# A fused attention and expert kernel: the fourth attention unit's keys and queries loaded sooner, and in the experts the second-layer weight chunks behind all transposes, with later splits and squares

## The chip, the cores and the metric

The kernel runs on one core of a Trainium2 chip. The metric is the device time of one execution in microseconds. The core's engines work side by side, each through its own list of instructions in order: PE (matrix multiplication), DVE (vector), ACT (scalar functions), POOL (here indexed gathers and scatters) and SP (here only the issue of DMA transfers). They wait for one another through semaphores.

## The reference, cut to what matters

```python
# attention: q, k, v of shape (8, 8, 576, 64); heads 0-3 banded, heads 4-7 strided
scores = (q @ k.T) / 8
mask_local   = (rel >= 0) & (rel < 32)
mask_strided = (rel >= 0) & (pos_k % 32 == pos_q % 32)
x = softmax(where(mask, scores, -1e9)) @ v          # x: 4608 tokens of 512
# experts: 8 of them, each takes at most 576 tokens
logits = x @ w_gate                                 # (4608, 8)
for (token, expert) in order of falling logit:
    if token is free and expert has fewer than 576: assign
for e in range(8):
    out[mine(e)] = relu(x[mine(e)] @ w1[e]) @ w2[e] # 512 -> 1024 -> 512
```

## The kernel before, in words

**Attention.** Each of the 8 batches has a strided and a banded part; these 16 *units* (`todo[0]` to `todo[15]`, strided first) are worked through in pairs of heads, two per unit, by one loop over `i`. Step `i` computes head pair `i` (`mix`, `norm`), the scores of pair `i + 1` and the first matmuls of pair `i + 2`. Loads go over SP's queue in the order in which the code writes them: `load_kq` takes keys (`ks` strided, `kl` banded) and queries (`qs`, `ql`) of one head pair, `load_v` the values (`v_s`, `v_l`). All go through `flow` (L255 to L262), which makes the first transfer of a group wait for a given mark, an instruction of an earlier unit, or else for the third group before it. Some small constants are loaded between them: `wg_sb` (the gate's weights), `sum_g` and `desc8h`. `drips` are small instructions tied to a step; one copies `wg_sb` into `wgp`, at step `GW_AT - 1`.

**Who gets which token.** The logits lead to a search, expert by expert, for the 576th largest logit among the free tokens. A round of `search` is a chain across engines: DVE compares all values with 17 candidates (`cm`, L844), PE counts (nine matmuls, L860), DVE folds (`red`, `r`), PE sums (L869), DVE tests against 576 (`g`, L876), PE sums (L879), DVE forms the next candidates (`cand`, L882). The search for expert e + 1 and the work for it runs between the matmuls of expert e.

**An expert.** Its tokens are gathered by POOL in five chunks of 128 rows, the last of 64 (`xr`, L1109). `halve` (L1095) splits each chunk into a high and a low half-precision part: ACT writes the high one (`xg`, L1098), DVE the low one (L1099), and SP issues a transposing DMA into `xt` (L1100). The weights come in quarters (`w`, L1012); their scale is found by four squares per layer on ACT (`jk`, L1032), a sum on DVE (`ss`, L1040), a matmul on PE (L1042) and a few small DVE operations (`ss_e`, `w_sw`). Then `split` cuts each layer into eight pieces, a high one on ACT (`w1h`, `w2h`, L1052) and a low one on DVE (`w1l`, `w2l`, L1053), which reads the high one. The first layer is 192 matmuls of 288 columns (L1208, in `hidden`), whose results ACT and DVE split into `hh` and `hl`; the second is L1256 (L1250 for the last 64 rows), whose results `y` POOL scatters to the output (L1267).

**What sets the order.** PE's order is that of the code: `ffn` yields its matmuls with their cost, `clock` adds these up, and chains of other work (search rounds, squares, scales, pieces, gathers) are advanced when their due time on this clock has come; numbers such as `T_SCALE` or `T_W` are the steps between them. On DVE and ACT a scheduler orders by priority, `urgent` raises it, and `follow(ins, others)` adds that `ins` is placed after the others, an order only and no wait. `bulk` uses it to put an instruction behind the last finished search count (`sums`), and `counted` puts what was issued shortly before a count behind it. `rush` holds the experts whose first layer has been reached.

Of the kernel before, what the change touches and what calls it, by code (L numbers as in the profile page):

```python
# [13 lines left out]
OP = mybir.AluOpType  # L14
# [19 lines left out]
B_LATE, L_AT, G5, GW_AT = 5, 8, 6, 4  # L34
# [27 lines left out]
CUT0, T_BEHIND, ROWS_BEHIND = 1, 1300, 3  # L62
# [76 lines left out]
def band_stride_attention_then_capacity_moe(ctx, tc, qt, kl, ks, nl, ns, wg, w1, w2, cst, out, dbg=None):  # L139
# [82 lines left out]
    with tc.tile_pool(name="ld", bufs=2) as ld, \  # L222
# [369 lines left out]
        flow([(wg_sb, wg), (sum_g, cst["sum_g"]), (desc8h, cst["desc_h"])])  # L592
# [34 lines left out]
        for i in range(-1, 2 * nu):  # L627
            u, n, m = pair(i), pair(i + 1), pair(i + 2)
            nu_ = todo[i // 2 + 3] if i >= 0 and i // 2 + 3 < nu else None
            kq_ = todo[i // 2 + 2] if i >= 2 and i // 2 + 2 < nu else None  # L630
# [29 lines left out]
            if nu_ and i % 2 == 0:  # L660
                nu_.load_v(1, n[0].top)
            elif kq_ and i % 2:
                kq_.load_kq(1, n[0].top)
            if u:
                u[0].mix(u[1], 1)
# [75 lines left out]
    lately, sums = [], []  # L741
# [94 lines left out]
    def search(rm, ohc, more):  # L836
        cand, src, top = cand0, rm, None
        ohv = ohc.rearrange("p c e -> p (c e)")
        for rd in range(R1):
            last = rd == R1 - 1  # L840
            t = cand[:, :J1] if last else cand[:, 1:J1 + 1]
            with urgent():
                cm = rt.tile([TP, NC, J1], F16, name="cm")
                nc.vector.tensor_tensor(cm, src[:, :, None].to_broadcast([TP, NC, J1]),  # L844
                                        t[:, None, :].to_broadcast([TP, NC, J1]), op=OP.is_ge)
# [157 lines left out]
    def weights(ph, ei):  # L1003
        e = nc.sync.value_load(ei[0:1, 0:1], min_val=0, max_val=E - 1)
        res, todo = [], []
        for name, w, nch, width, bits in (("w1", w1, DC, FF, W1_BITS), ("w2", w2, FC, DM, W2_BITS)):
# [43 lines left out]
            def split(c, f, k, wf=wf, sc=sc, hi=hi, lo=lo):  # L1050
                s_ = sc.bitcast(F32)[:, 0:1]
                nc.scalar.activation(hi[:, c, f], wf[:, c, f], AF.Copy, scale=s_)  # L1052
                nc.vector.scalar_tensor_tensor(lo[:, c, f], wf[:, c, f], s_, hi[:, c, f], op0=OP.mult,  # L1053
                                               op1=OP.subtract)
# [25 lines left out]
        g = spread(ph, [(T_W, lambda: None)] + sq1 + sc1 + cut1)  # L1080
# [13 lines left out]
    def halve(ph, xt, xr, t, n):  # L1094
        xg = xp.tile([128, 2 * DM], F16, name="xg", bufs=5)  # L1095
        xs, xv = xg[:n].rearrange("q (a j d) -> q j a d", a=2, j=2), xr[:n].rearrange("q (a d) -> q a d", a=2)
        with urgent(ph):
            nc.scalar.activation(xs[:, 0], xv, AF.Copy)  # L1098
            bulk(ph if t < ROWS_BEHIND else 0, nc.vector.tensor_tensor(xs[:, 1], xv, xs[:, 0], op=OP.subtract))  # L1099
# [87 lines left out]
    def fetch(ph, slot, wts):  # L1187
        idx, sx = yield from indices(ph, slot)
        xt, todo = tokens(ph, idx)
        for t, f in enumerate(todo):  # L1190
            yield T_ROWS if t == 0 else T_ROW
            f()
            if t >= NT - 3:
                wts[2]({NT - 3: (0,), NT - 2: (1,), NT - 1: (2, 3)}[t])
# [99 lines left out]
    with tc.manual_schedule(engines=MAN):  # L1294
        work[0] = now[:4] + (now[4](),)
        chains.append([T_LOAD0, load0()])
        for ph in range(E):
            with tc.manual_schedule(engines=MAN0) if ph in MANP else nullcontext():
# [5 lines left out]
                lately.clear()  # L1304
                for c in list(chains):
# [77 lines left out]
```

## Time and profile before

| | |
|---|---|
| three runs | 675.93 us median (670.42, 676.23, 675.93) |
| profiled execution | 676.45 us |
| its span, first to last instruction | 674.7 us |
| mean granted clock of PE | 0.957 |
| PE busy | 603.6 us, 89% |
| DVE, ACT, POOL busy | 454.7, 332.6, 108.7 us |
| DMA | 102.40 MB, mean 152 GB/s |
| first layers (L1208), 1536 matmuls | 291.0 us of PE |
| second layers (L1256), 768 matmuls | 290.9 us of PE |

The busy times of matmuls overlap one another, since they are pipelined. In the rows below a time in square brackets is the idle time of the engine just before the instruction, with what ended it. "issue" means that nothing in the profile shows what the engine waited for; SPq is SP's queue of DMA issues.

### The profile page before, as it was taken

What the parts mean: (1) busy time and instruction counts of PE and PEld (TensorE: products, weight loads), DVE (VectorE), ACT (ScalarE), POOL (GpSimd) and SP (SyncE); (2) the same over time, 40 slices, a digit from 0 to 9 for tenths busy, and PEclk for the clock granted to TensorE, in tenths of its full rate; (3) what the DMA queues carried; (4) which work ended last, traced back from release to release, by engine and by line L of the source; (5) the groups of instructions that cost most, each with busy time, mean ns of one, the idle gap of its engine ahead of it and who ended that gap; (6) DMA issues with size and microseconds to landing.
All of it is one profiled execution on the core that took longest, in us unless ns stands there. A gap on an engine that the chain in (4) does not pass through costs nothing.

```text
span 674.7 us, 19417 instructions
## 1 busy us (share of the span) xinstructions
PE 603.6 (89%) x8128; PEld 395.4 (59%) x8128; DVE 454.7 (67%) x1381; ACT 332.6 (49%) x554; POOL 108.7 (16%) x124
## 2 busy tenths in 40 slices
PE   8789999998947699979999989989998999899993
PEld 4566667766733565457457448547646746646741
DVE  4757778877777888729768776975965956650600
ACT  2555554545302564535655456554565456843510
POOL 2001101111101100400330150051052031211011
PEclk9879999999966899979999999999999999899998
DMA  9868888887314503840590493375257089641010
GB/s 240 202 211 228 233 230 238 248 223 214 111 38 177 167 1 141 193 128 14 181 254 15 149 200 113 141 158 162 111 128 224 20 233 332 142 149 48 1 40 32
DMA packets 76363, 102.40 MB, mean 152 GB/s; under 512 B 41292, under 2 KB 49062, under 8 KB 75763
## 3 DMA queue, kind: packets, MB, share of 16 engines
q1 hardware_dynamic: 68195, 79.61, 41.7%
q0 software_dynamic: 7360, 21.15, 10.7%
q8 instruction: 64, 1.05, 0.7%
q10 hardware_dynamic: 720, 0.39, 0.2%
q14 instruction: 24, 0.20, 0.1%
HBM read 73.60 MB, written 18.87 MB: 137 GB/s over the span
## 4 chain that ended last, share of the span: by engine, by line
PE 17%; issue 15%; DVE 15%; DMA 10%; POOL 4%; ACT 4%; SPq 0%; POOLq 0%; DVEq 0%; ACTq 0%
PE ph L1208 12%; DMA w<-in_w_dram 5%; DVE w2l L1053 3%; PE ph L1256 3%; POOL xr L1109 3%; DMA xr<-x_scr,idx 3%; DVE hl L1216 2%; DVE w1l L1053 2%; DMA xt<-xg 2%; DVE cm L844 1%; ACT jk L1032 1%; POOL out_dram L1267 1%; DVE xg L1099 1%; ACT hh L1215 1%; DMA out_dram<-y,idx 1%
## 5 line engine op out<-in xcount | busy, mean ns | idle before, releaser
L1208 PE MATMUL ph<-xt,w1h 128*128 128x288 f16 (+2 forms) x1024 | 178.9, 290 | 6.8 <-DMA xt<-xg 4.8
L1208 PEld LDWEIGHTS <-w1h 128*128 128x128 f16 x1024 | 97.9, 99 | 36.2 <-issue 5.7
L1208 PE MATMUL ph<-xt,w1l 128*128 128x288 f16 (+2 forms) x512 | 112.1, 290 | 0.0
L1267 POOL DMA_INDIRECT out_dram<-y,idx x40 | 47.3, 1181 | 339.5 <-ACT y L1266 317.5
L1256 PE MATMUL ph<-w2l,hh 128*128 128x512 f16 x256 | 96.9, 379 | 0.4 <-DVE w2l L1053 0.4
L1256 PE MATMUL ph<-w2h,hh 128*128 128x512 f16 x256 | 97.0, 379 | 0.0
L1256 PE MATMUL ph<-w2h,hl 128*128 128x512 f16 x256 | 97.0, 379 | 0.0
L1032 ACT ACTIVATE jk<-w 128x1024 f16<-128x1024 f32 x64 | 67.4, 1054 | 56.5 <-DMA w<-in_w_dram 55.3
L1215 ACT ACTIVATE hh<-ph 128x576 f16<-128x576 f32 (+2 forms) x72 | 42.7, 592 | 81.9 <-PE ph L1208 81.1
L1256 PEld LDWEIGHTS <-hh 128*128 128x128 f16 x512 | 49.1, 98 | 57.4 <-issue 6.7
L1216 DVE SCALAR_TENSOR_TENSOR hl<-ph,hh 128x576 f16<-128x576 f32 (+2 forms) x72 | 49.5, 687 | 47.6 <-ACT hh L1215 47.3
L1208 PEld LDWEIGHTS <-w1l 128*128 128x128 f16 x512 | 50.7, 99 | 14.1 <-issue 1.4
L378 ACT ACTIVATE pr<-spa 128x576 f32<-128x576 f32 x32 | 20.8, 651 | 61.9 <-PE spa L375 45.2
L1053 DVE SCALAR_TENSOR_TENSOR w1l<-w,w_sw,w1h 128x512 f16<-128x512 f32 x64 | 46.1, 745 | 4.8 <-ACT w1h L1052 4.8
L1109 POOL DMA_INDIRECT xr<-x_scr,idx x40 | 41.5, 1038 | 46.8 <-DVE L L953 25.3
L1052 ACT ACTIVATE w1h<-w,w_sw 128x512 f16<-128x512 f32 x64 | 42.2, 710 | 13.0 <-DVE w_sw L210 11.9
L1266 ACT ACTIVATE y<-ph,so 128x512 f32<-128x512 f32 x32 | 21.8, 681 | 53.4 <-PE ph L1256 53.3
L1053 DVE SCALAR_TENSOR_TENSOR w2l<-w,w_sw,w2h 128x512 f16<-128x512 f32 x64 | 46.8, 746 | 0.4 <-ACT w2h L1052 0.3
L1052 ACT ACTIVATE w2h<-w,w_sw 128x512 f16<-128x512 f32 x64 | 42.2, 711 | 8.1 <-DVE w_sw L210 8.1
L1256 PEld LDWEIGHTS <-hl 128*128 128x128 f16 x256 | 24.9, 97 | 29.8 <-issue 4.0
L429 POOL DMA_DIRECT2D x_scr<-xs x23 | 15.1, 661 | 159.2 <-DVE vsum L298 101.7
L1099 DVE TENSOR_TENSOR xg<-xr,xg 128x512 f16<-128x512 f32 (+1 forms) x37 | 24.8, 685 | 15.1 <-ACT xg L1098 14.9
(619 smaller groups left out, 929.7 us busy)
## 6 DMA issues: line engine op xcount, KB each, us to landing
w<-in_w_dram SPq DMA_DIRECT2D x64, 512.0 KB
kl<-in_kl_dram SPq DMA_DIRECT2D x16, 304.0 KB
v_s<-in_ns_dram SPq DMA_DIRECT2D x16, 292.5 KB
v_l<-in_nl_dram SPq DMA_DIRECT2D x16, 292.5 KB
ks<-in_ks_dram SPq DMA_DIRECT2D x16, 288.0 KB
qs<-in_qt_dram SPq DMA_DIRECT2D x16, 288.0 KB
ql<-in_qt_dram SPq DMA_DIRECT2D x16, 288.0 KB
x_scr<-xl SPq DMA_DIRECT2D x8, 512.0 KB
```

Source lines behind the costliest of these rows:

```text
L378: nc.scalar.activation(pr[:, :S].rearrange("k (h n) -> k h n", h=2), u.sp[p][:, :, :HS], AF.Exp, scale=0.125)
L1032: ins = nc.scalar.activation(jk, wf[:, c * n4:(c + 1) * n4].rearrange("p c f -> p (c f)"), AF.Square, scale=1.41422, accum_out=sq[:, c:c + 1])
L1052: nc.scalar.activation(hi[:, c, f], wf[:, c, f], AF.Copy, scale=s_)
L1053: nc.vector.scalar_tensor_tensor(lo[:, c, f], wf[:, c, f], s_, hi[:, c, f], op0=OP.mult, op1=OP.subtract)
L1099: bulk(ph if t < ROWS_BEHIND else 0, nc.vector.tensor_tensor(xs[:, 1], xv, xs[:, 0], op=OP.subtract))
L1109: nc.gpsimd.indirect_dma_start(out=xr[:n], out_offset=None, in_=x_rows, in_offset=bass.IndirectOffsetOnAxis(ap=idx[:n, t:t + 1], axis=0))
L1208: nc.tensor.matmul(tile_[:, j, :w], wt[:, d, f * 128:(f + 1) * 128], xt[:, d // 2, xx, d % 2, c], start=(k == 0), stop=(k == 3 * DC - 1))
L1215: evicted.append(nc.scalar.activation(hv, src, AF.Relu))
L1216: nc.vector.scalar_tensor_tensor(lv, src, 0.0, hv, op0=OP.max, op1=OP.subtract)
L1256: nc.tensor.matmul(py, a[:, f, ts_], w[:, f], start=(k == 0), stop=(k == len(todo) - 1))
L1266: nc.scalar.activation(y, py, AF.Copy, scale=so[:, t:t + 1])
L1267: st = nc.gpsimd.indirect_dma_start(out=out_rows, out_offset=bass.IndirectOffsetOnAxis(ap=idx[:n, t:t + 1], axis=0), in_=y[:n], in_offset= ...
```

## The change

**Attention.** Keys and queries of the fourth unit (`todo[3]`, banded part of batch 1) are loaded at step 1, both head pairs, instead of at steps 2 and 3; the general rule starts at step 4. The three small constants go behind them instead of ahead of the loop, and `wgp` is copied at step 5 instead of 3.

**Experts.** (1) The quarters of the second-layer weights are issued by `fetch` after its last transpose, not between the last three. (2) In experts 1 to 6 the pieces from the seventh on (sixth on in expert 1), while the expert is not in `rush`, have their low part placed after the last finished search count, and pieces issued within 4000 of a count's due time are placed after that count. (3) The DVE half of the last row chunk is placed after the latest comparison `cm`. (4) The first layer's scale is due 2800 after its squares, not 1500, and the squares of expert 7's first layer start 15000 after its weights, not 4000.

```diff
--- before.py
+++ after.py
@@ -31,7 +31,7 @@
 OPEN_S, OPEN_L = 1, 3
 DEPTH = 3
 WARM = {(-2, 0): 11, (-1, 0): 3, (-1, 2): 3}
-B_LATE, L_AT, G5, GW_AT = 5, 8, 6, 4
+B_LATE, L_AT, G5, GW_AT = 5, 8, 6, 6
 V_AT, V_AT_S, COPY_AT = 5, 4, (-3, -5, -2, -4, -1, -4)
 VW = D + 1
 LR = 3 * 32 + E
@@ -59,7 +59,7 @@
 T_HOT6, T_CLOSE6 = 3200, 9000
 T_W21, T_SCALE2, T_CUT2 = (3200, 300, 3000, 3000), 2600, 1250
 T_F, T_LOAD0, T_HOT1, T_W, T_SQ, T_SCALE, T_CUT, T_BULK0 = 3000, 1500, 6350, 4000, 1500, 1500, 1500, 600
-CUT0, T_BEHIND, ROWS_BEHIND = 1, 1300, 3
+CUT0, T_BEHIND, ROWS_BEHIND, PIECES, T_TAIL, T_SCALE1, T_W7 = 1, 1300, 3, 6, 4000, 2800, 15000
 EDGE0, PEAKS, PEAKS_N = 18, (24, 29), (1, 3)
 FIRST_AT = (3, 4)
 LATE_Q, STORE_Q = (2, 3), (3, 4, 5)
@@ -589,7 +589,6 @@
         for p in range(2):
             todo[2].load_kq(p)
             todo[2].load_v(p)
-        flow([(wg_sb, wg), (sum_g, cst["sum_g"]), (desc8h, cst["desc_h"])])
         last = 2 * nu - 1
         edge = (B - 2) * S // TP
 
@@ -627,7 +626,7 @@
         for i in range(-1, 2 * nu):
             u, n, m = pair(i), pair(i + 1), pair(i + 2)
             nu_ = todo[i // 2 + 3] if i >= 0 and i // 2 + 3 < nu else None
-            kq_ = todo[i // 2 + 2] if i >= 2 and i // 2 + 2 < nu else None
+            kq_ = todo[i // 2 + 2] if i >= 4 and i // 2 + 2 < nu else None
             if nu_ and i % 2 == 0:
                 nu_.load_v(0, todo[0].top if i == 0 else todo[i // 2 - 1].done)
             late_constants(i)
@@ -661,6 +660,8 @@
                 nu_.load_v(1, n[0].top)
             elif kq_ and i % 2:
                 kq_.load_kq(1, n[0].top)
+            elif i == 1:
+                todo[3].load_kq(0, n[0].top)
             if u:
                 u[0].mix(u[1], 1)
             warm(i, 1)
@@ -674,6 +675,9 @@
                 u[0].norm(u[1])
             if kq_ and i % 2 == 0:
                 kq_.load_kq(0, u[0].done)
+            elif i == 1:
+                todo[3].load_kq(1, u[0].done)
+                flow([(wg_sb, wg), (sum_g, cst["sum_g"]), (desc8h, cst["desc_h"])])
             for f in mids3.get(i, []):
                 f(a, b)
             if n:
@@ -738,7 +742,7 @@
     def urgent(ph=1):
         return tc.high_priority(offset=URGENT * (2 if ph == 0 else 1))
 
-    lately, sums = [], []
+    lately, sums, cms, pieces = [], [], [], []
 
     def bulk(ph, ins):
         if ph and ph not in rush:
@@ -746,6 +750,10 @@
             lately.append((due_now(), ins))
 
     def counted(red, total):
+        while pieces:
+            t, ins = pieces.pop()
+            if t > due_now() - T_TAIL:
+                follow(ins, (total,))
         while lately:
             t, ins = lately.pop()
             if t > due_now() - T_BEHIND:
@@ -841,8 +849,8 @@
             t = cand[:, :J1] if last else cand[:, 1:J1 + 1]
             with urgent():
                 cm = rt.tile([TP, NC, J1], F16, name="cm")
-                nc.vector.tensor_tensor(cm, src[:, :, None].to_broadcast([TP, NC, J1]),
-                                        t[:, None, :].to_broadcast([TP, NC, J1]), op=OP.is_ge)
+                cms.append(nc.vector.tensor_tensor(cm, src[:, :, None].to_broadcast([TP, NC, J1]),
+                                                 t[:, None, :].to_broadcast([TP, NC, J1]), op=OP.is_ge))
                 cv = cm.rearrange("p c j -> p (c j)")
                 n = 1 if rd == R1 - 2 else J1 + 1
                 if not last:
@@ -1050,8 +1058,11 @@
             def split(c, f, k, wf=wf, sc=sc, hi=hi, lo=lo):
                 s_ = sc.bitcast(F32)[:, 0:1]
                 nc.scalar.activation(hi[:, c, f], wf[:, c, f], AF.Copy, scale=s_)
-                nc.vector.scalar_tensor_tensor(lo[:, c, f], wf[:, c, f], s_, hi[:, c, f], op0=OP.mult,
-                                               op1=OP.subtract)
+                ins = nc.vector.scalar_tensor_tensor(lo[:, c, f], wf[:, c, f], s_, hi[:, c, f], op0=OP.mult,
+                                                     op1=OP.subtract)
+                if ph and ph not in rush and k >= PIECES - (ph == 1):
+                    follow(ins, sums[-1:])
+                    pieces.append((due_now(), ins))
 
             todo.append([(T_SQ, lambda c=c, g=square: g(c)) for c in range(4)])
             todo.append([(T_SCALE, scale)])
@@ -1077,7 +1088,7 @@
                 return g
 
             return res, (start, more, later)
-        g = spread(ph, [(T_W, lambda: None)] + sq1 + sc1 + cut1)
+        g = spread(ph, [(T_W if ph < E - 1 else T_W7, lambda: None)] + sq1 + [(T_SCALE1, sc1[0][1])] + cut1)
         chains.append([due_now(), g])
         thirds[ph] = evenly([(t, f) for t, (_, f) in zip(T_W21, sq2)] + [(T_SCALE2, sc2[0][1])] + [(T_CUT2, f) for _, f in cut2])
         return res, g, later
@@ -1096,7 +1107,11 @@
         xs, xv = xg[:n].rearrange("q (a j d) -> q j a d", a=2, j=2), xr[:n].rearrange("q (a d) -> q a d", a=2)
         with urgent(ph):
             nc.scalar.activation(xs[:, 0], xv, AF.Copy)
-            bulk(ph if t < ROWS_BEHIND else 0, nc.vector.tensor_tensor(xs[:, 1], xv, xs[:, 0], op=OP.subtract))
+            ins = nc.vector.tensor_tensor(xs[:, 1], xv, xs[:, 0], op=OP.subtract)
+            if t < ROWS_BEHIND:
+                bulk(ph, ins)
+            elif 0 < ph < E - 1 and t == NT - 1:
+                follow(ins, cms[-1:])
             turned.append(nc.sync.dma_start_transpose(xt[:, :, t * 128:t * 128 + n], xg[:n]))
 
     def tokens(ph, idx):
@@ -1190,8 +1205,7 @@
         for t, f in enumerate(todo):
             yield T_ROWS if t == 0 else T_ROW
             f()
-            if t >= NT - 3:
-                wts[2]({NT - 3: (0,), NT - 2: (1,), NT - 1: (2, 3)}[t])
+        wts[2](range(4))
         yield T_LOAD - T_ROWS
         work[ph] = wts[0], xt, idx, sx, wts[1]
         ready.add(ph)
@@ -1302,6 +1316,7 @@
                     advance(c)
                 rush.add(ph)
                 lately.clear()
+                pieces.clear()
                 for c in list(chains):
                     if c[1] is work[ph][4]:
                         c[0] = clock
```

The rows show where instructions stand. First SP, attention, the loads of the third to fifth unit, as a difference (`v_l_147`, `kl`, `ql` are the fourth unit's, `v_s_139` the third's, `v_s_135` the fifth's):

```order
 L262 DMA v_s_139<-in_ns_dram 6x1560
+L262 DMA v_l_147<-in_nl_dram 32x2340 x2
+L262 DMA kl<-in_kl_dram 128x608
+L262 DMA ql<-in_qt_dram 128x576
+L262 DMA kl<-in_kl_dram 128x608
+L262 DMA ql<-in_qt_dram 128x576
 L262 DMA wg_sb<-in_wg_dram 128x32
 L262 DMA sum_g<-in_c_sum_g_dram 128x8
 L262 DMA desc8h<-in_c_desc_h_dram 128x8
-L262 DMA v_l_147<-in_nl_dram 32x2340 x2
-L262 DMA v_s_135<-in_ns_dram 48x1560
-L262 DMA v_s_135<-in_ns_dram 6x1560
```

The removed rows go on with the rest of the fifth unit's values and the fourth unit's `kl`, `ql`, `kl`, `ql`. These four stand ahead of the constants and of the fifth unit's values now.

SP again, the last stretch of expert 1's loading, before (`w_4794` are its second-layer quarters):

```order
L1100 DMA_TRANSPOSE xt<-xg 128x8x128 x3
L1012 ISA
L1012 DMA w_4794<-in_w_dram 128x2x512
L1100 DMA_TRANSPOSE xt<-xg 128x8x128
L1012 ISA
L1012 DMA w_4794<-in_w_dram 128x2x512
L1100 DMA_TRANSPOSE xt<-xg 128x8x64
L1012 ISA
L1012 DMA w_4794<-in_w_dram 128x2x512
L1012 ISA
L1012 DMA w_4794<-in_w_dram 128x2x512
```

and after:

```order
L1115 DMA_TRANSPOSE xt<-xg 128x8x128 x4
L1115 DMA_TRANSPOSE xt<-xg 128x8x64
L1020 ISA
L1020 DMA w_4794<-in_w_dram 128x2x512
L1020 ISA
L1020 DMA w_4794<-in_w_dram 128x2x512
```

All five transposes stand ahead of the second-layer quarters now, of which two are shown. In experts 2 to 5 that was the order before, too; in expert 6 it changes as here.

DVE, expert 3, from the first row chunk to the third round's comparison `cm`, before (numbers tell the chunks apart; `xg_6701` is the last one):

```order
L1099 TENSOR_TENSOR xg_6622<-xr_6557,xg_6622 128x2x256
L1099 TENSOR_TENSOR xg_6638<-xr_6559,xg_6638 128x2x256
L876 TENSOR_SCALAR g1_6630,ih1_6631<-pr__6602 128x8
L1099 TENSOR_TENSOR xg_6657<-xr_6561,xg_6657 128x2x256
L1099 TENSOR_TENSOR xg_6674<-xr_6563,xg_6674 128x2x256
L882 SCALAR_TENSOR_TENSOR cand18_6646<-steps_3772,pr__6602,pre1_6578 128x18
L1099 TENSOR_TENSOR xg_6701<-xr_6565,xg_6701 64x2x256
L844 TENSOR_TENSOR cm_6648<-rmn_6384,cand18_6646 128x612
L852 TENSOR_SCALAR pre1_6650<-steps_3772,cand18_6646 128x18
L1053 SCALAR_TENSOR_TENSOR w1l_6325<-w1_6317,w_sw1_6323,w1h_6324 128x4x128 x2
```

and after, where the last chunk is `xg_6697`:

```order
L1110 TENSOR_TENSOR xg_6620<-xr_6548,xg_6620 128x2x256
L1110 TENSOR_TENSOR xg_6636<-xr_6550,xg_6636 128x2x256
L1110 TENSOR_TENSOR xg_6655<-xr_6552,xg_6655 128x2x256
L884 TENSOR_SCALAR g1_6630,ih1_6631<-pr__6602 128x8
L1110 TENSOR_TENSOR xg_6671<-xr_6554,xg_6671 128x2x256
L1061 SCALAR_TENSOR_TENSOR w1l_6325<-w1_6317,w_sw1_6323,w1h_6324 128x4x128
L890 SCALAR_TENSOR_TENSOR cand18_6644<-steps_3772,pr__6602,pre1_6578 128x18
L1061 SCALAR_TENSOR_TENSOR w1l_6325<-w1_6317,w_sw1_6323,w1h_6324 128x4x128
L852 TENSOR_TENSOR cm_6646<-rmn_6384,cand18_6644 128x612
L860 TENSOR_SCALAR pre1_6648<-steps_3772,cand18_6644 128x18
L1110 TENSOR_TENSOR xg_6697<-xr_6556,xg_6697 64x2x256
L1061 SCALAR_TENSOR_TENSOR w1l_6325<-w1_6317,w_sw1_6323,w1h_6324 128x4x128
```

`cm` stands ahead of the last chunk now, and two pieces `w1l` stand between the fourth chunk and `cm`; `g` stands behind the third chunk instead of the second.

ACT at the same place, before:

```order
L1052 ACTIVATE w1h_6324<-w1_6317,w_sw1_6323 128x4x128 x5
L1266 ACTIVATE y_6591<-ph_6470,so_5973 128x512
L1098 ACTIVATE xg_6622<-xr_6557 128x2x256
L1098 ACTIVATE xg_6638<-xr_6559 128x2x256
L1098 ACTIVATE xg_6657<-xr_6561 128x2x256
L1098 ACTIVATE xg_6674<-xr_6563 128x2x256
L1052 ACTIVATE w1h_6324<-w1_6317,w_sw1_6323 128x4x128
L1098 ACTIVATE xg_6701<-xr_6565 64x2x256
L1052 ACTIVATE w1h_6324<-w1_6317,w_sw1_6323 128x4x128 x2
```

and after:

```order
L1060 ACTIVATE w1h_6324<-w1_6317,w_sw1_6323 128x4x128 x3
L1280 ACTIVATE y_6589<-ph_6470,so_5973 128x512
L1109 ACTIVATE xg_6620<-xr_6548 128x2x256
L1109 ACTIVATE xg_6636<-xr_6550 128x2x256
L1109 ACTIVATE xg_6655<-xr_6552 128x2x256
L1109 ACTIVATE xg_6671<-xr_6554 128x2x256
L1109 ACTIVATE xg_6697<-xr_6556 64x2x256
L1060 ACTIVATE w1h_6324<-w1_6317,w_sw1_6323 128x4x128 x4
L1280 ACTIVATE y_6660<-ph_6592,so_5973 128x512
```

Before, five pieces `w1h` stand ahead of the row chunks and one between the fourth chunk and the last; after, three stand ahead and five behind the last chunk.

## The prediction, made before the changed kernel ran

> **What bounds the kernel now.** I read the page first: the matrix engine (PE) is busy for 603.6 of 674.7 us, so it sets the time, and a change can only win where PE stands still or runs at the lower clock. Then I looked for PE's idle time, for what ended it, and for the granted clock around it.
>
> ```profile
> PE 603.6 (89%) x8128; PEld 395.4 (59%) x8128; DVE 454.7 (67%) x1381; ACT 332.6 (49%) x554; POOL 108.7 (16%) x124
> ```
>
> The rows of the second view cut PE's time into pieces of 3.41 us (the length of the shortest stretch at half clock), laid so that clock changes fall on their borders. Four places are shown: attention, expert 1, expert 3, experts 6 and 7. Columns: from and to, length, busy time of PE, PEld, DVE, ACT, POOL, granted clock, DMA share, GB/s.
>
> ```profile
> 36.89:40.30 3.41, 0.86 (x27) 0.70 (x27) 0.00 (x0) 0.60 (x2) 0.00 (x0) 1.00 0.96 350
> 40.30:43.71 3.41, 3.41 (x70) 2.91 (x70) 2.77 (x11) 1.84 (x3) 0.00 (x0) 0.50 0.20 70
> 43.71:47.12 3.41, 3.41 (x58) 3.00 (x56) 2.17 (x7) 2.74 (x4) 0.00 (x0) 0.50 0.59 178
> ...
> 286.06:289.47 3.41, 0.03 (x1) 0.00 (x0) 0.23 (x2) 0.12 (x1) 0.97 (x1) 1.00 1.10 290
> 289.47:292.88 3.41, 2.55 (x11) 1.65 (x12) 0.00 (x0) 0.00 (x0) 0.00 (x0) 0.50 1.07 403
> 292.88:296.29 3.41, 3.41 (x23) 2.36 (x21) 0.39 (x2) 0.00 (x0) 0.00 (x0) 0.50 0.00 0
> ...
> 395.28:398.69 3.41, 1.45 (x7) 0.49 (x5) 1.72 (x4) 2.12 (x5) 0.00 (x0) 1.00 1.14 202
> 398.70:402.11 3.41, 2.88 (x22) 1.42 (x23) 2.64 (x9) 0.50 (x1) 2.43 (x1) 1.00 1.18 194
> ...
> 576.19:579.60 3.41, 1.47 (x15) 0.96 (x13) 1.34 (x5) 3.38 (x7) 2.50 (x4) 1.00 0.71 204
> 579.60:583.01 3.41, 3.41 (x16) 2.16 (x15) 2.46 (x5) 2.14 (x5) 0.64 (x1) 0.50 0.75 196
> ```
>
> So PE's idle time is paid twice in places. A piece in which PE worked only 0.86, 0.03 or 1.47 us is followed by one or two at clock 0.50, each of which does half its work: about 1.7 us lost. The limit lies near 1.45 us busy: at 395 that much kept the full clock, at 576 1.47 lost it.
>
> The Trainium skill, "TensorE: Matmul & The Clock Gate" (Part 1, and "HAM oscillation"), has the clock as either half or full, decided over free-running windows of 3413 ns, which these rows show; but its rule asks for no idle gap above some 3.4 us, and the row at 576 lost the clock with 1.94 us idle. By that rule the clock term of the experts below would be nothing and the sum 2.7 us lower; the rows speak against it.
>
> **The change part by part**, against the profiled execution (676.45 us, span 674.7), 0.5 us above the median 675.93.
>
> *Attention: keys and queries of the fourth unit sooner.*
>
> ```profile
> 27.39 2.33 SPq L262 DMA_DIRECT2D v_s<-in_ns_dram  x4
> 29.82 0.35 SPq L262 DMA_DIRECT2D kl<-in_kl_dram  x1
> ...
> 37.50 0.43 PE L352 MATMUL spa<-ql,kl 64*64 64x32 f32 x16 [0.64 <-DMA ql<-in_qt_dram]
> 39.87 0.32 PE L352 MATMUL spa<-ql,kl 64*64 64x32 f32 x8 [1.93 <-issue]
> ```
>
> The four loads (SP ql and kl) leave the queue ahead of four v_s loads and three small ones, whose issue alone took 2.33 us; PE's wait of 0.64 for ql ends, since they come at least that much earlier. The values of the fifth unit, now behind them, are not used until two units later. The next wait, 1.93 us, names no data ("issue"), so I leave it. Then the piece at 36.89 would have PE busy for 1.5 us, right at the limit. I give the two half-clock pieces behind it (3.4 us) one chance in three to go: -0.6 - 1.1 = **-1.7**. Ends: 0 (the wait moves to "issue") and -0.6 - 1.9 - 3.4 = -5.9. The gate weights' copy, two steps later, feeds only the logits at the end of the attention.
>
> *Expert 1: second-layer weights behind all transposes.*
>
> ```profile
> 276.91 5.27 SPq L1100 DMA_TRANSPOSE xt<-xg  x3
> 282.37 1.18 SPq L1012 DMA_DIRECT2D w<-in_w_dram  x1
> 283.65 1.32 SPq L1100 DMA_TRANSPOSE xt<-xg  x1
> 285.17 0.44 SPq L1012 DMA_DIRECT2D w<-in_w_dram  x1
> 285.71 1.34 SPq L1100 DMA_TRANSPOSE xt<-xg  x1
> ...
> 281.91 0.68 DVE L1099 TENSOR_TENSOR xg<-xr,xg 64x512 f16<-64x512 f32 x1
> ...
> 285.81 0.28 PE L1208 MATMUL ph<-xt,w1h 128*128 128x288 f16 x1 [0.36 <-DMA xt<-xg]
> 290.33 0.90 PE L1208 MATMUL ph<-xt,w1h 128*128 128x288 f16 x3 [4.23 <-DMA xt<-xg]
> ...
> 285.71 4.57 DMA xt<-xg
> ```
>
> The fifth transpose's rows were halved at 282.59 (281.91 + 0.68), but it was issued at 285.71, behind two weight loads (1.18 + 0.44). After: the fourth follows the third at 282.2, the fifth at 283.6 (+1.32). Expert 3, where no load stood between, took 3.81 instead of 4.57 (its row is below), so it lands at 287.2 to 287.4 instead of 290.3: **-3.0**. PE still waits some 1.4 us, with over 2 us busy in any piece, so I take the half clock of 289.47 to 296.29 to go: (2.55 + 3.41)/2 = **-3.0**. Ends: -2 and -7. The first two loads moved back start some 2.5 us later and are first read by squares that stand behind the expert's first hidden tile; if they came too late, the second layer's scale would, at the price of the stall in expert 6 below (1.9). Only this expert and the sixth change here; in experts 2 to 5 all five transposes stood ahead of these loads already.
>
> *Experts 2 to 5: pieces and last row chunk.* The wait that this is about: first the chain in expert 3, with the counts (L860) of the four experts in the middle:
>
> ```profile
> 392.05 4.70 DMA xr<-x_scr,idx
> ...
> 396.77 0.63 ACT L1098 ACTIVATE xg<-xr 64x512 f16<-64x512 f32 x1 [1.29 <-DMA xr<-x_scr,idx]
> 397.31 1.32 ACT L1052 ACTIVATE w1h<-w,w_sw 128x512 f16<-128x512 f32 x2
> ...
> 397.44 0.68 DVE L1099 TENSOR_TENSOR xg<-xr,xg 64x512 f16<-64x512 f32 x1 [1.69 <-ACT xg L1098]
> 398.04 0.78 DVE L844 TENSOR_TENSOR cm<-rmn,cand 128x612 f16<-128x612 f32 x1
> 398.89 1.41 DVE L1053 SCALAR_TENSOR_TENSOR w1l<-w,w_sw,w1h 128x512 f16<-128x512 f32 x2
> ...
> 342.88 0.47 PE L860 MATMUL pr__5919<-ohn,cm 128*68 128x32 f16 x9 [0.86 <-DVE cm L844]
> 398.88 0.47 PE L860 MATMUL pr__6684<-ohn,cm 128*68 128x32 f16 x9 [2.15 <-DVE cm L844]
> 453.28 0.47 PE L860 MATMUL pr__7449<-ohn,cm 128*68 128x32 f16 x9 [1.70 <-DVE cm L844]
> 507.93 0.47 PE L860 MATMUL pr__8214<-ohn,cm 128*68 128x32 f16 x9 [2.00 <-DVE cm L844]
> ...
> 399.32 3.81 DMA xt<-xg
> ```
>
> PE waits for cm, cm for the last xg, that for the fifth gather, landed at 396.75. The change puts cm ahead of that xg. But it also puts the fourth and fifth w1l ahead of cm, and their w1h behind the last xg on ACT. So cm still waits for the fifth gather, over a longer way: ACT xg from 396.77, w1h from 397.31 and 397.92 (1.32 for two), w1l on DVE from 398.03 and 398.7 (0.70 each), cm from 399.45 instead of 398.04, counts at 400.3: +1.4. The last xg comes behind cm (400.25), the last transpose is issued at 400.95 and lands 3.81 later, at 404.8 instead of 403.1: +1.7. Against this the index chain no longer stands behind the scale's small operations on PE and DVE, so the gathers start a little sooner; no single row prices that, and I take it at some 0.3 (an estimate). Left: +1.3 for each of four experts, **+5.2**. Ends: 0 each (the gather, whose landing took 4.70, comes 1.3 sooner) and +1.7.
>
> PE's idle stretch at these counts grows from 2.15 to about 2.9 us (+1.1 from the counts, -0.6 that is spent earlier, since g of the round before comes behind a third xg, +0.3 because PE arrives sooner), in experts 4 and 5 to 2.5 and 2.8 and in expert 2 to 1.7. Laid at random on pieces of 3.41 us with a limit of 2.0 to 2.2 us idle, that is a chance of about a half in three experts: 1.6 pieces at half clock, 1.7 us each: **+2.7**. Ends 0 and four times two pieces, +13.6.
>
> *Experts 6 and 7: later squares and scale.*
>
> ```profile
> L1256 PE MATMUL ph<-w2l,hh 128*128 128x512 f16 x256 | 96.9, 379 | 0.4 <-DVE w2l L1053 0.4
> ...
> L1032 ACT ACTIVATE jk<-w 128x1024 f16<-128x1024 f32 x64 | 67.4, 1054 | 56.5 <-DMA w<-in_w_dram 55.3
> ...
> 578.81 0.22 DVE L1040 TENSOR_REDUCE ss<-sq 128x1 bf16<-128x4 f32 x2 [1.46 <-ACT jk L1032]
> ...
> 579.02 0.18 PE L1042 MATMUL pr__9204<-ss,ones_b 128*128 128x1 bf16 x1 [1.94 <-DVE ss L1040]
> ```
>
> The scale of expert 6's second layer (ss) comes in DVE's order only when eight squares are through, four of which are expert 7's, at 1.05 us each. With those four behind it, ss is ready some 4 us sooner, ahead of PE. The stall of 1.94 goes, and the half-clock piece at 579.60 (-1.7). In the order the second layer's pieces now also stand together, so its first matmuls should not wait (0.4 before, of which I take 0.3): 1.94 + 1.7 + 0.3 = **-3.9**. Expert 7's own squares, scale and pieces now fall into expert 6's second layer, in which DVE and ACT have nothing else that PE waits for; if they filled it to its end, expert 7's first layer would wait for a piece, 0.7 us. Ends: -1.9 and -4.2. The scale at 2800 in the other experts moves w1h by a few matmuls, with no wait at its end but the one counted.
>
> **Sum:** -1.7 - 3.0 - 3.0 + 5.2 + 2.7 - 3.9 = -3.7. On the profiled execution 672.7, on the median 672.2: I forecast **672.3 us**. The kernel before spreads over 6 us in three runs (670.42 to 676.23), so 1% (6.8 us) is about what a measurement can tell from no change.
>
> **Rivals.** *Faster, the clock holds.* No half clock in experts 2 to 5 and the attention's stretch recovered: -0.6 - 3.4 - 6.0 + 5.2 - 3.9 = -8.7, 667.5. For it: 1.45 us busy kept the clock there. Against: longer stalls than any of those. *Faster, cm comes free.* If the fifth gather landed over 2 us sooner, so that cm is ready when PE comes, the four stalls (0.86, 2.15, 1.70, 2.00) would go, -6.7 instead of +7.9: -18.3, 658. Against: the order puts cm behind w1l pieces that need ACT behind the same gather. *Slower.* The longer idle stretch in experts 2 to 5 costs two pieces at half clock each (as after 286): decided where less than 1.4 us of a piece is busy, all four: +13.6 + 5.2, with -0.6 - 3.0 - 1.9 of gains: +13.3, 689; with three of them, 686. *Little is left*: the gains stand at their lower ends (0, 2.0 and 1.9) against +5.2: +1.3, 677.5.
>
> **Chances.** Forecast 0.45 (666 to 678), clock holds 0.24, cm free 0.09, slower 0.14, little left 0.08. Faster by over 1%: 0.24 + 0.09 and a little of the forecast's lower side, 0.37; slower by over 1%: 0.14 and a sliver, 0.15; within: 0.48. The range leaves out the end of "cm free" below and of "slower" above: 661 to 684.
>
> **What would show it.** In the profile after: the row of expert 1's wait for xt at 1 to 1.5 us and clock 1.00 around it; the counts (cm) in experts 2 to 5 with waits of 2.5 to 3 us and the last transpose issued right behind the last xg; no wait for ss near 577; unit 4's ql wait gone near 36.9. I am wrong if the waits for cm shrink, if the clock drops elsewhere (search rounds, attention), or if the weight loads behind the transposes make the squares late.

## The result and the profile after

| | before | changed |
|---|---|---|
| median of 22 runs | 676.02 us (667.24 to 684.81) | 682.55 us (673.14 to 694.36, and one of 1429.52) |
| ratio | | 1.012, 95% interval 1.0089 to 1.0151 |
| profiled execution, span | 676.45, 674.7 us | 676.2, 674.4 us |

The change makes the kernel about 1.2% slower. Executions of one kernel differ by some 3%, the one of 1429.52 us aside; the ratios leave out those over 1.5% above the kernel's fastest, so they differ a little from the quotient of the medians. The profiled execution of the changed kernel lies 6 us under its median, so its span says little; its waits say what happened. First the third round's counts in experts 2 to 5 (timeline of PE: start, length, instruction, idle before and what ended it), then the same counts in a second profiled execution (run 12), of 687.75 us:

```profile
336.70 0.47 PE L868 MATMUL pr__5915<-ohn,cm 128*68 128x32 f16 x9 [3.33 <-DVE cm L852]
394.18 0.72 PE L868 MATMUL pr__6680<-ohn,cm 128*68 128x32 f16 x9 [4.33 <-DVE cm L852]
452.27 0.47 PE L868 MATMUL pr__7445<-ohn,cm 128*68 128x32 f16 x9 [2.73 <-DVE cm L852]
508.15 0.47 PE L868 MATMUL pr__8210<-ohn,cm 128*68 128x32 f16 x9 [3.22 <-DVE cm L852]
```

```profile
346.11 0.72 PE L868 MATMUL pr__5915<-ohn,cm 128*68 128x32 f16 x9 [4.51 <-DVE cm L852]
403.67 0.47 PE L868 MATMUL pr__6680<-ohn,cm 128*68 128x32 f16 x9 [3.47 <-DVE cm L852]
461.12 0.47 PE L868 MATMUL pr__7445<-ohn,cm 128*68 128x32 f16 x9 [3.30 <-DVE cm L852]
519.85 0.58 PE L868 MATMUL pr__8210<-ohn,cm 128*68 128x32 f16 x9 [3.87 <-DVE cm L852]
```

Before, these waits were 0.86, 2.15, 1.70 and 2.00, together 6.7 us; now they are 13.6 and 15.2 us. A second wait stands ahead of them: PE waits for `g` of the round before, 0.76, 1.20, 0.53 and 0.72 us in the first profile, where before it did not wait there at all. The new order has `g` behind the third row chunk; the prediction took 0.6 us for it. Expert 3 before, then changed:

```profile
393.52 0.17 PE L879 MATMUL pr__6602<-ih,ones_j 128*128 128x1 f16 x1
```

```profile
386.64 0.16 PE L887 MATMUL pr__6602<-ih,ones_j 128*128 128x1 f16 x1 [1.20 <-DVE g L884]
```

Both kinds together are 6.7 us before and 16.8 and 18.8 us in the changed kernel. The chain of expert 3 in the changed kernel (first profile) shows the way that the prediction read from the order, step for step:

```profile
384.80 5.76 DMA xr<-x_scr,idx
...
390.57 0.03 ACT xg L1109
...
391.11 0.71 ACT w1h L1060
391.82 0.03 issue
391.85 0.75 DVE w1l L1061
392.60 0.15 DVE cand L890
392.75 0.66 DVE w1l L1061
393.42 0.72 DVE cm L852
394.13 0.04 issue
394.18 0.72 PE pr__6680 L868 x9
```

From the last gather's landing to cm it takes 2.8 us (390.57 to 393.33 in DVE's timeline), against 2.7 forecast and 1.3 before (396.77 to 398.04). What had not been forecast stands in the first row: the gather itself took 5.76 us from issue to landing instead of 4.70.

The other waits that were to go did go in this trace. Expert 1's transposes stand together, its wait for xt is 1.41 us instead of 4.23, and the wait for ql at the fourth unit is gone (the largest idle time near there is the one "issue" row):

```profile
274.25 8.25 SPq L1115 DMA_TRANSPOSE xt<-xg  x5
282.69 2.15 SPq L1020 DMA_DIRECT2D w<-in_w_dram  x4
...
284.17 0.54 PE L1222 MATMUL ph<-xt,w1h 128*128 128x288 f16 x3 [1.41 <-DMA xt<-xg]
...
578.25 0.17 PE L1050 MATMUL pr__9199<-ss,ones_b 128*128 128x1 bf16 x1
...
32.98 0.69 PE L450 MATMUL spb<-ident,xs 54*128 54x54 f32 x11 [2.32 <-issue]
```

The row at 578 is expert 6's second-layer scale: no wait stands ahead of it any more.

Then the clock. The view by stretches of 3.41 us again, called windows from here on, so that they are not taken for the pieces of the weights. First profile of the changed kernel (from and to, length, busy time of PE, PEld, DVE, ACT, POOL, granted clock, DMA share, GB/s):

```profile
331.89:335.30 3.41, 1.48 (x7) 0.49 (x5) 1.32 (x4) 2.20 (x4) 0.00 (x0) 1.00 1.13 215
335.31:338.72 3.41, 2.02 (x18) 1.13 (x19) 3.38 (x8) 2.05 (x4) 1.69 (x1) 1.00 0.40 89
...
389.92:393.33 3.41, 0.00 (x0) 0.00 (x0) 1.48 (x3) 2.75 (x5) 0.00 (x0) 1.00 1.21 189
393.33:396.75 3.42, 2.58 (x14) 1.27 (x15) 3.38 (x9) 1.51 (x3) 1.88 (x1) 0.50 0.44 92
396.75:400.16 3.41, 3.41 (x10) 1.23 (x9) 0.60 (x3) 0.00 (x0) 0.00 (x0) 0.50 0.83 221
...
447.94:451.35 3.41, 1.60 (x8) 0.51 (x6) 1.41 (x3) 2.68 (x5) 0.00 (x0) 1.00 1.17 235
451.35:454.77 3.42, 2.50 (x20) 1.32 (x21) 3.39 (x9) 1.58 (x3) 1.88 (x1) 1.00 0.33 66
...
505.97:509.39 3.42, 1.24 (x14) 0.77 (x15) 3.42 (x7) 2.84 (x5) 0.91 (x1) 1.00 0.63 135
509.39:512.80 3.41, 3.41 (x11) 1.22 (x10) 1.81 (x7) 0.00 (x0) 0.96 (x1) 0.50 0.67 189
```

Where a wait falls across a border (experts 2 and 4) no window is empty enough and the clock stays; where most of it falls into one (experts 3 and 5), the next is at half, in expert 3 the next two. In the second profile each of the four waits emptied a window, PE busy for 0.00, 0.34, 0.91 and 0.21 us, and the next was at half. Expert 2:

```profile
342.57:345.98 3.41, 0.00 (x0) 0.00 (x0) 2.20 (x5) 3.41 (x6) 0.00 (x0) 1.00 1.18 170
345.98:349.39 3.41, 3.28 (x16) 1.57 (x17) 3.09 (x8) 0.79 (x2) 1.88 (x1) 0.50 0.47 103
```

### The profile page after: what moved, and what is told of

The parts are those of the page before. It is cut to its first block, busy times and chain, and to the rows that moved or that the text cites. A ratio compares the mean times of both kernels' runs of the same rounds, so it can differ in the third digit from the quotient of the medians.

```text
span 674.4 us, 19407 instructions
## 1 busy us (share of the span) xinstructions
PE 601.7 (89%) x8125; PEld 392.4 (58%) x8128; DVE 456.5 (68%) x1381; ACT 332.1 (49%) x554; POOL 107.2 (16%) x124
## 3 DMA queue, kind: packets, MB, share of 16 engines
q0 software_dynamic: 7360, 21.15, 10.9%
## 4 chain that ended last, share of the span: by engine, by line
PE 31%; issue 14%; DVE 11%; POOL 4%; DMA 4%; ACT 3%; POOLq 0%; DVEq 0%; ACTq 0%
PE ph L1222 15%; PE ph L1270 11%; DMA xr<-x_scr,idx 3%; POOL xr L1124 3%; DVE w2l L1061 2%; PE ph L1264 2%; DVE hl L1230 2%; DVE cm L852 1%; POOL out_dram L1281 1%; DVE w1l L1061 1%; ACT hh L1229 1%; ACT w2h L1060 1%; DMA xt<-xg 0%; ACT w1h L1060 0%; DVE xg L1110 0%
## 5 line engine op out<-in xcount | busy, mean ns | idle before, releaser
L1222 PE MATMUL ph<-xt,w1h 128*128 128x288 f16 (+2 forms) x1024 | 176.8, 288 | 3.9 <-DVE xt L1103 1.4
L1270 PE MATMUL ph<-w2h,hh 128*128 128x512 f16 x256 | 98.8, 386 | 1.5 <-DVE hl L1230 1.5
L1281 POOL DMA_INDIRECT out_dram<-y,idx x40 | 44.7, 1118 | 347.4 <-ACT y L1280 328.1
L1270 PE MATMUL ph<-w2l,hh 128*128 128x512 f16 x256 | 98.6, 385 | 0.7 <-DVE w2l L1061 0.7
L1270 PE MATMUL ph<-w2h,hl 128*128 128x512 f16 x256 | 98.7, 385 | 0.3 <-DVE ss_e L205 0.3
L1061 DVE SCALAR_TENSOR_TENSOR w1l<-w,w_sw,w1h 128x512 f16<-128x512 f32 x64 | 45.5, 744 | 11.6 <-ACT w1h L1060 11.5
```

Source lines behind the costliest of these rows:

```text
L1061: ins = nc.vector.scalar_tensor_tensor(lo[:, c, f], wf[:, c, f], s_, hi[:, c, f], op0=OP.mult, op1=OP.subtract)
L1222: nc.tensor.matmul(tile_[:, j, :w], wt[:, d, f * 128:(f + 1) * 128], xt[:, d // 2, xx, d % 2, c], start=(k == 0), stop=(k == 3 * DC - 1))
L1270: nc.tensor.matmul(py, a[:, f, ts_], w[:, f], start=(k == 0), stop=(k == len(todo) - 1))
L1281: st = nc.gpsimd.indirect_dma_start(out=out_rows, out_offset=bass.IndirectOffsetOnAxis(ap=idx[:n, t:t + 1], axis=0), in_=y[:n], in_offset= ...
```

## The experiments

Theory A: the later scale of the first layer puts the pieces w1h behind the last row chunk on ACT, and cm stands behind their w1l. Theory C: the longer waits are paid twice, through the clock. Rival B: the order that puts cm ahead of the last chunk is to blame. Rival D: the last gather's own late landing is. All ratios are to the kernel before on the same chip, with 95% intervals.

**1. The whole change with the scale at 1500.**

```diff
-T_SCALE1 = 2800
+T_SCALE1 = 1500
```

> The whole change, but the first layer's scale due 1500 after its squares as before. On ACT five w1h then stand ahead of the row chunks and one between the fourth and the last, and only that one's w1l stands between the fourth chunk and cm, so cm no longer waits for the last gather. Theory A (the later scale pushes the pieces that cm stands behind past the last gather): the waits before the counts of the third round in experts 2 to 5 fall from 2.7 to 4.3 us to below 0.5, and the time is 10 to 18 us under the kernel before (ratio 0.973 to 0.986). Rival B (putting the last row chunk behind cm makes its transpose late, whatever the scale): a wait for xt ahead of the first layers takes their place, ratio 1.000 to 1.012.

Measured: 0.9959 (0.9922 to 0.9997), between the two expectations. The 1.6% that the change lost beyond this hang on one number, as Theory A has it. But no 10 to 18 us were gained: the waits for cm fall to 0.37 to 0.61 us, and waits for xt stand at the first layers (2.14, 1.77, 0.76, 2.15 us), 6.8 us together, as much as the waits for cm before. Rival B's mechanism is there too: the transposes are the next thing to be late:

```profile
342.65 0.54 PE L1222 MATMUL ph<-xt,w1h 128*128 128x288 f16 x3 [2.14 <-DMA xt<-xg]
```

**2. The scale at 2800 alone**, in the kernel before.

```diff
+T_SCALE1 = 2800
...
-        g = spread(ph, [(T_W, lambda: None)] + sq1 + sc1 + cut1)
+        g = spread(ph, [(T_W, lambda: None)] + sq1 + [(T_SCALE1, sc1[0][1])] + cut1)
```

> The kernel before with only the scale due at 2800 instead of 1500. ACT has the last chunk ahead of five pieces w1h, DVE the last chunk, then one w1l, then cm. Theory A: longer waits for cm in experts 2 to 5 (2.5 to 4 us instead of 0.9 to 2.2), slower than before by 6 to 14 us, ratio 1.009 to 1.021. Rival B: as before, 0.997 to 1.003.

Measured: 1.0142 (1.0091 to 1.0193). The time is as Theory A has it: this part alone costs what the whole change lost. The waits for cm are so only in part. Two of the four are about 2 us, as before, and expert 4's 4.82 us comes from a fifth gather that took 6.90 us to land; together they are 11.3 us against 6.7. PE also waits for g, 3.9 us in experts 2 to 5, and three windows behind the counts are at half clock:

```profile
444.76 6.90 DMA xr<-x_scr,idx
...
339.38 0.47 PE L864 MATMUL pr__5917<-ohn,cm 128*68 128x32 f16 x9 [2.58 <-DVE cm L848]
396.17 0.47 PE L864 MATMUL pr__6682<-ohn,cm 128*68 128x32 f16 x9 [1.94 <-DVE cm L848]
454.61 0.72 PE L864 MATMUL pr__7447<-ohn,cm 128*68 128x32 f16 x9 [4.82 <-DVE cm L848]
511.87 0.47 PE L864 MATMUL pr__8212<-ohn,cm 128*68 128x32 f16 x9 [1.99 <-DVE cm L848]
```

**3. Filling the wait.**

```diff
+if rd == 2 and len(closed) in (3, 4, 5, 6):
+    for _ in range(24):
+        nc.tensor.matmul(pr[:, 256:], warm_i[:, :128], warm_i[:, :256], start=True, stop=True,
+                         skip_group_check=True)
```

> The changed kernel with 24 matmuls of zeros (256 columns, some 2.6 us in all, results unused) on PE ahead of the third round's counts in experts 2 to 5, where PE waits 2.7 to 4.3 us. They fill the wait, not shorten it. Theory C (the stall is paid a second time through the clock): no half clock behind these counts, 3 to 10 us under the changed kernel, ratio 0.997 to 1.007 to the kernel before. Rival (the stalls alone): as the changed kernel, 1.012, or slower where the fill is longer than the stall.

Measured: 1.0013 (0.9975 to 1.0051) against 1.012 without the fill: 1.07%, 7.2 us back (by the two intervals 3.9 to 10.5), with cm no earlier. That supports Theory C: about half of what the waits cost was the clock. In the profile the fill is the row of 24 (2.78 us); behind it PE waits 1.52 us in expert 3, and the clock holds there and in experts 4 and 5. In expert 2 the wait was too long for the fill: 2.33 us were left, and the clock was lost against the expectation (window at 338.03 at half; a second-layer matmul takes 0.63 us there, 0.38 at full clock):

```profile
393.43 2.78 PE L869 MATMUL pr__6704<-warm_i 128*128 128x256 bf16 x24
397.73 0.47 PE L871 MATMUL pr__6704<-ohn,cm 128*68 128x32 f16 x9 [1.52 <-DVE cm L852]
...
338.12 0.72 PE L871 MATMUL pr__5915<-ohn,cm 128*68 128x32 f16 x9 [2.33 <-DVE cm L852]
339.06 0.63 PE L1273 MATMUL ph<-w2h,hl 128*128 128x512 f16 x1
```

This execution (677.0 us) shows the clock held, but not the whole gain: its waits for cm, fill included, are longer than in the changed kernel's first profile (16.1 against 13.6 us), and from expert 2's count on it is at most 3 us shorter than the changed kernel's two. The 7.2 us rest on the ratios.

**4. The attention's part alone**, in the kernel before.

```diff
-B_LATE, L_AT, G5, GW_AT = 5, 8, 6, 4
+B_LATE, L_AT, G5, GW_AT = 5, 8, 6, 6
...
-        flow([(wg_sb, wg), (sum_g, cst["sum_g"]), (desc8h, cst["desc_h"])])
...
-            kq_ = todo[i // 2 + 2] if i >= 2 and i // 2 + 2 < nu else None
+            kq_ = todo[i // 2 + 2] if i >= 4 and i // 2 + 2 < nu else None
...
+            elif i == 1:
+                todo[3].load_kq(0, n[0].top)
...
+            elif i == 1:
+                todo[3].load_kq(1, u[0].done)
+                flow([(wg_sb, wg), (sum_g, cst["sum_g"]), (desc8h, cst["desc_h"])])
```

> The kernel before with only the attention's part: the fourth unit's keys and queries sooner, constants behind them. The prediction's term: 0.6 us of wait and one chance in three for 3.4 us of half clock, ratio 0.993 to 1.000. Rival: the profile after has the search start 4.9 us sooner; if that is this part and not the clock's luck, ratio 0.990 to 0.994.

Measured: 1.0007 (0.9971 to 1.0043). It brings nothing that can be told. The 4.9 us by which the search began sooner in the profile after (its first count at 186.75 instead of 191.65) were not its doing: in run 5's profile, without this part, it begins at 185.25, and in the second profile of the changed kernel at 194.64. Over all profiles of this case it begins at 184.26 to 194.64 with this part and at 185.25 to 191.65 without.

**5. The weights behind the transposes alone.**

```diff
-            if t >= NT - 3:
-                wts[2]({NT - 3: (0,), NT - 2: (1,), NT - 1: (2, 3)}[t])
+        wts[2](range(4))
```

> The kernel before with only the second-layer weight quarters behind the last transpose. The prediction's term: expert 1's wait for xt falls from 4.2 to 4.8 us to some 1.4, -3.0, and the half clock behind it goes, 1.7 or 3.0 more: ratio 0.991 to 0.996. Rival: later weights make the second layer's scale late, 0.998 to 1.003.

Measured: 0.991 (0.9873 to 0.9947), 6.1 us, as expected. In its profile expert 1 waits 1.31 us for xt, with no half clock behind it. Expert 6, whose order changes too, had no wait for xt of 0.5 us or more before and has none here.

**6. Expert 7's later squares alone.**

```diff
+T_W7 = 15000
...
-(T_W, lambda: None)
+(T_W if ph < E - 1 else T_W7, lambda: None)
```

> The kernel before with only expert 7's first squares 15000 behind its weights instead of 4000. The prediction's term: PE's wait for ss of expert 6's second layer (1.5 to 1.9 us) goes, and the half clock behind it where there is one: -1.9 to -3.9, ratio 0.994 to 0.997. Rival: the splits of both layers meet later, and waits of 0.7 to 1.5 us in expert 6's second layer give it back: 0.998 to 1.002.

Measured: 1.0005 (0.9967 to 1.0042). The wait for ss and the half clock behind it are gone in its profile, too, but at most 2.2 us of the time went with them. The rival of the expectation has it: waits of 0.58 (ss of expert 7), 0.68 (hl), 0.19 and 0.52 (w2l) and 0.30 us (hl) now stand around the start of expert 6's second layer, 2.3 us together, where before there were 1.94 and 0.44. Two of expert 7's squares stand on ACT right ahead of the last `hh`, which `hl` needs:

```profile
587.33 1.06 ACT L1036 ACTIVATE jk<-w 128x1024 f16<-128x1024 f32 x1
...
588.38 0.63 ACT L1223 ACTIVATE hh<-ph 128x576 f16<-128x576 f32 x1
...
589.95 0.38 PE L1264 MATMUL ph<-w2h,hh 128*128 128x512 f16 x1 [0.68 <-DVE hl L1224]
```

The half clock that went is hidden in this execution by two other windows at half, behind the counts of experts 4 and 5 (from 452.65 and 507.26).

**7. These three parts together, without the scale and the two orders** (from the changed kernel).

```diff
-T_SCALE1 = 2800
+T_SCALE1 = 1500
...
-                if ph and ph not in rush and k >= PIECES - (ph == 1):
+                if False:
...
-            elif 0 < ph < E - 1 and t == NT - 1:
-                follow(ins, cms[-1:])
```

> The change without its later scale and without the two orders on DVE (pieces behind sums, last row chunk behind cm): attention, weights behind transposes and expert 7's late squares are left. If the scale and the orders brought nothing: as the change with the scale at 1500, ratio 0.990 to 0.996. If the orders on DVE are what made that one faster: 0.996 to 1.000.

Measured: 0.9895 (0.985 to 0.994), median 664.71 us, just under the first expected range. This beats both kernels by about what the weights alone gave (run 5). Against run 1 it says that the two orders cost some 0.6% rather than gain, though with 0.6% either way by the two intervals that is barely clear of noise.

**8. The two orders alone**, in the kernel before.

```diff
+                if ph and ph not in rush and k >= PIECES - (ph == 1):
+                    follow(ins, sums[-1:])
+                    pieces.append((due_now(), ins))
...
+            elif 0 < ph < E - 1 and t == NT - 1:
+                follow(ins, cms[-1:])
```

> The kernel before with only the two orders on DVE: cm ahead of the last row chunk, with its w1h ahead of the last chunk on ACT. By the run with the scale at 1500, PE's waits for cm (0.9 to 2.2 us) go and waits for xt of about the same length (0.8 to 2.2 us) come at the first layers: 0.997 to 1.003. Rival: cm's waits were the bound, and 5 us go: 0.990 to 0.994.

Measured: 1.0154 (1.0082 to 1.0226), outside both expectations. The median of its six executions is 691.59 us, 2.8% over that of the kernel before on this chip (672.6), and the ratio rests on the two shortest (680.03 and 685.03 us): the sign is plain, the size is not. The profiled execution took 692.88 us. The likely reason stands in SP's queue. With cm ahead of the last chunk, that chunk's transpose comes so late that a weight quarter is put ahead of it, in experts 2 to 5 too, and PE waits for xt 3.45, 2.92, 3.91 and 3.47 us:

```profile
396.32 6.67 SPq L1111 DMA_TRANSPOSE xt<-xg  x4
403.19 0.43 SPq L1016 DMA_DIRECT2D w<-in_w_dram  x1
403.73 1.94 SPq L1111 DMA_TRANSPOSE xt<-xg  x1
...
408.88 0.90 PE L1219 MATMUL ph<-xt,w1h 128*128 128x288 f16 x3 [2.92 <-DMA xt<-xg]
```

The waits for cm are 0.40 to 0.47 us here. So the orders seem to need the weights behind the transposes; with them (run 1) they are nearly harmless.

**9. cm ahead of the pieces**, all else as changed: the direct trial of Theory A.

```diff
+                if ph > 1 and ph not in rush and k in (3, 4):
+                    follow(ins, cms[-1:])
```

> The changed kernel with one more order: the fourth and fifth w1l of experts 2 to 6 are placed behind the latest cm. DVE then has the fourth chunk, cand, cm, the last chunk, three w1l. Theory A (cm waits for the last gather through these two pieces): PE's waits for cm of 2.7 to 4.3 us fall to below 0.8, waits for xt of some 2 us come at the first layers, ratio 0.994 to 1.001 (with the scale at 1500 it was 0.996). Rival D (the last gather itself lands later, 5.2 us behind its issue against 4.3 before, and everything waits for it): waits for xt of 3 to 4 us, 1.004 to 1.012.

Measured: 0.9928 (0.989 to 0.9966), against 1.012: two pieces behind cm instead of ahead of it are worth 13 us (1.9%), more than expected. PE's waits for cm fall to 0.28, 0.35, none and 1.14 us, the last above the expected 0.8. cm follows the fourth chunk at once, while the last gather still lands late (6.21, 4.18, 4.86, 6.58 us from issue to ACT's read), so Rival D alone is not what decided. The expected waits for xt did not come; the late gather costs the next round's sum (`r`) 1.06 to 2.6 us instead. Waits for g, cm and r are 13 us in experts 2 to 5, against 16.8 in the changed kernel's first profile, and one window there is at half instead of three, so part of the 13 us is the clock. Expert 3:

```profile
386.12 0.24 DVE L890 SCALAR_TENSOR_TENSOR cand<-steps,pr__6602,pre 128x18 f32<-128x18 f32 x1
386.39 0.80 DVE L852 TENSOR_TENSOR cm<-rmn,cand 128x612 f16<-128x612 f32 x1
387.10 0.23 DVE L860 TENSOR_SCALAR pre<-steps,cand 128x18 f32<-128x18 f32 x1
387.24 0.68 DVE L1112 TENSOR_TENSOR xg<-xr,xg 64x512 f16<-64x512 f32 x1
387.85 2.06 DVE L1061 SCALAR_TENSOR_TENSOR w1l<-w,w_sw,w1h 128x512 f16<-128x512 f32 x3
...
387.24 0.47 PE L868 MATMUL pr__6680<-ohn,cm 128*68 128x32 f16 x9 [0.35 <-DVE cm L852]
390.29 0.17 PE L877 MATMUL pr__6680<-r,fold 68*128 68x8 f16 x1 [1.06 <-DVE r L874]
```

**10. Run 7 with the scale at 1900.**

```diff
-T_SCALE1 = 1500
+T_SCALE1 = 1900
```

> Attention, weights behind transposes and late squares of expert 7 (0.9895 with the scale at 1500 and no orders), with the scale due 1900 behind its squares. In experts 2 to 5 the index matmuls stand ahead of the scale's, and ACT keeps four w1h ahead of the chunks and one ahead of the last. If sooner indices help: 0.983 to 0.989. If gathers only land later when issued sooner (rival D): 0.989 to 0.994.

Measured: 0.9874 (0.9815 to 0.9933). No difference from run 7 can be told, so this does not decide between the two expectations. In its profile the waits for cm are 0.86, 3.05, 1.77 and 2.37 us, against 0.81, 1.73, 0.82 and 1.75 in run 7's.

**11. Run 7 with a short fill.**

```diff
+if rd == 2 and len(closed) in (3, 4, 5, 6):
+    for _ in range(10):
+        nc.tensor.matmul(pr[:, 256:], warm_i[:, :128], warm_i[:, :256], start=True, stop=True,
+                         skip_group_check=True)
```

> The same three parts without scale and orders, with 10 matmuls of zeros (256 columns, 1.1 us, results unused) on PE ahead of the third round's counts in experts 2 to 5, where PE waits 0.8 to 1.75 us. Theory C (waits near 2 us lose the clock in some executions): 0 to 3 us under that kernel, 0.985 to 0.990. Rival: 0.990 to 0.993, by the little that fills longer than a wait cost.

Measured: 0.9899 (0.9839 to 0.9959), not to be told from run 7's 0.9895; a gain of up to 3 us lies within the intervals. Run 7's profile has no half clock behind its waits of 0.8 to 1.75 us to save. Run 5's profile, with waits of 2.13 and 2.31 us in experts 3 and 5, has one window at half behind each.

**12. The changed kernel again**, with no edit.

> The changed kernel once more: its first profiled execution (676.2 us) lies 6 us under its median. Theory C: in an execution near the median (682.6) the same waits stand in experts 2 to 5, with more pieces at half clock behind them (five or more instead of three). Rival: the waits themselves are longer.

Measured: 687.75 and 676.26 us. Both expectations hold in part: four windows at half clock behind the counts, one for each expert, instead of three (not five or more), and waits of 15.2 instead of 13.6 us. The rest of the 11.5 us between the two profiles lies mostly in the attention, whose end (the start of the search) comes 7.9 us later, with five windows more at half clock.

## Why the prediction was wrong

The forecast was a gain of 3.7 us; measured is a loss of 8 us (1.2% of 676). The mechanism in experts 2 to 5 was read rightly from the order, with its sign; its size was not, and that term decides the sign of the whole. Of the 12 us between forecast and measurement, some 7 lie there; most of the rest are two gains, in attention and in experts 6 and 7, that did not come.

- **Experts 2 to 5, the failed step.** Forecast +5.2 for the chain and +2.7 for the clock, 7.9 together. Measured between run 7 and the changed kernel: 0.9895 against 1.012, 15 us (by the two intervals 11.5 to 19; experts 1 and 6, which the scale and the orders touch too, are in it). Run 1 against the changed kernel gives the scale's share, 1.6% or 10.9 us; the orders' is 0.6% or 4.3 us.
- *The chain.* I let the gathers start 0.3 us sooner and land as before, that is, I put their landing at nothing. They landed later: 5.40, 5.77, 4.57 and 5.25 us from issue to ACT's read, against 3.44, 4.72, 4.28 and 4.58 before, 4.0 us together. So PE's waits for cm were 3.3, 4.3, 2.7 and 3.2 instead of 1.7, 2.9, 2.5 and 2.8, and its idle time for g and cm grew by 10.1 us (12.1 in the second profile) instead of 5.2. Why the gathers land later stays open (last section).
- *The clock.* 7.2 us (run 3), not 2.7. I had a chance of about a half in three experts that a wait of 2.5 to 2.9 us empties a window, 1.6 windows in all. With the longer waits it was three and four windows in the two profiles, 5.1 and 6.8 us at 1.7 each. The rule of the Trainium skill, "TensorE: Matmul & The Clock Gate" (Part 1), is that gaps above some 3.4 us cost the clock. These traces do not agree: waits of 3.22 and 3.30 us lost it here, as 1.94 did before, and one of 3.33 us, across a border, kept it.
- **Expert 1** (forecast -6.0): right. Run 5 measured -6.1 us (its interval: 3.6 to 8.5 us of gain), and the wait for xt of 1.41 us was in the forecast (1.4).
- **Attention** (-1.7): nothing measured (run 4, at most 2 us). The wait that named ql went, but the neighbouring "issue" wait and the clock go their own way from execution to execution.
- **Experts 6 and 7** (-3.9): the stall went as forecast, the time hardly (run 6, at most 2.2 us). I took it that ACT and DVE had nothing else there that PE waits for; they had `hh` and `hl`, and waits of 2.3 us took the place of 2.4 (2.5 in the changed kernel's first profile: 1.45, 0.19, 0.52 and 0.29).
- **Rivals.** "Slower" saw the right place, with 0.14, but not the later gather, and it had eight windows at half where the profiles show three and four: that its 686 to 689 us came nearer than the forecast is partly luck. "cm comes free" fell: the gather landed later, not sooner, and where cm is made nearly free otherwise (run 1), xt is late by as much.

## What to carry to other kernels

A delay given to an instruction off the critical path (here a scale, 1.3 us later) moves everything that hangs on it past something else in the engines' ordered lists; look in the order for what now stands between a late arrival and the chain that PE waits for. Price a wait on PE by its length and by where it can empty a clock window, for beyond some 2 us the second may cost as much as the first (run 3: 7.2 of some 15 us). A part that looks best in one profiled execution may be the execution's luck; try it alone.

## What the runs showed of the hardware

- An execution's clock windows lie at a different place each time, and waits that recur can fall in step with them: in run 12 the half-clock windows began at 345.98, 404.01, 462.03 and 520.06, 58.03 us apart, which is 17 times 3.413.
- The limit for losing the clock is not sharp in PE's busy time: windows with 1.45, 1.48 and 1.60 us busy kept it, 1.47, 1.24 and 0.91 lost it. Over the fourteen profiles of this case, every window at full clock with PE busy for less than 1.43 us was followed by one at half. In the experts (from 240 us on) the highest that lost it was 1.64, in run 10; in the attention windows with up to 2.5 us busy lost it too. The last 15 us of each execution are left out.
- In the fourteen profiles (experts 2 to 5, 56 cases) the last gather was read 3.4 to 5.1 us after its issue (median 4.5) where the first transpose was issued 0.5 us behind it (35 cases), and 4.1 to 6.9 (median 5.4) where that came at the same time or up to 1.1 us ahead (21 cases). Of these 21, 20 are from kernels with the scale at 2800. That the transposes slow the gather was not tried by itself.
